# Attention of the first two batches ahead of the dense layer, and each decoded weight chunk used for both batches

## The chip, the cores and the metric

The kernel runs on one core of a Trainium2 chip. The metric is the device time of one execution in microseconds (us). The engines are TensorE (PE in the rows; PEld is its weight load), ScalarE (ACT), VectorE (DVE), GpSimd (POOL) and SyncE (SP); SPq, ACTq and POOLq are their instruction queues where they issue DMAs.

## The reference

Four batches of 448 tokens pass through attention with a sigmoid, a dense layer with a leaky rectifier, and a layer of eight experts, one for each token.

```python
def _attn_ref(q, k, v):                     # (4, 12, 448, 64) each
    scores = scale * np.matmul(q, k.transpose(0, 1, 3, 2)) - np.log(S)
    return np.matmul(1.0 / (1.0 + np.exp(-scores)), v)

def _moe_ref(x, w_in, w_out):               # 1792 x 768, 768 x 2048, 2048 x 768
    h = x @ w_in
    return np.maximum(0.01 * h, h) @ w_out

def _moe2_ref(x, w_gate, w_output_gate, w1, w2):   # 8 experts, 768 x 1024 x 768
    e_idx = np.argmax(x @ w_gate, axis=1)          # one expert for each token
    out[mask] = gate_w * eom * (np.maximum(x[mask] @ w1[e], 0.0) @ w2[e])
```

w_in and w_out arrive as 64-bit floats. All other inputs are 32-bit.

## The kernel before, in words

*Products.* Each product of float32 values is three fast matmuls: `mm3` multiplies the high part of the weights (`whi`) with the high and the low part of the activations, and the low part (`wlo`) with the high part. A weight chunk is up to six blocks of 128x128. ScalarE casts it to `whi`, VectorE subtracts to get `wlo`; five raw chunks, three high and three low ones fit.

*Decoding.* A chunk of w_in or w_out is read as pairs of 32-bit words into one of five places (`r64x`, `r64big`), in two pieces of up to three blocks. ScalarE shifts the exponent (`dw`), VectorE puts the bits together in three operations (lines 1176, 1179, 1182), and the result goes into a raw tile and by a POOL DMA also into the scratch tensor `wscr`, from which later batches read it.

*Attention.* A batch has six pairs of heads. A pair has two halves, FRONT and BACK, of two score tiles each (`sc`). A half is one piece of PE work (`both`): the scores of this half, then the values (`pv`) of the half before. ScalarE makes the sigmoid (`at`) of a score tile, which frees it; two score tiles fit, and one tile of values. When a pair's values are complete, ScalarE casts them to the high part of x (`x0h`, `x1h`) and VectorE subtracts. Batch 0 loads k and q by rows and turns them on PE (`pst`); later batches load them in blocks of 32 columns, four DMAs for each of k and q, and turn them on VectorE (`kt`, `qt`). `TURNED` sets the first batch that does so.

*Stages.* `first_batches` lists the operations of attention 0, attention 1 and dense 0 (16 hidden tiles `f`, then 6 outer tiles `d`) with durations, due times and the tiles they use. `_Plan.order` plays them through with these durations: at each step the engine that is free first takes the ready operation with the earliest due time. Its order is the order in which the instructions are written, and each engine then works through its own in that order. Two banks (`ps_m`) hold dense sums. Behind it, `gen_M1` and `gen_M2` write the dense layer of batch 1, with the routing of batch 0 as a side job; then come the experts (`gen_M3`, `gen_M4`) beside attention 2, and the same for batches 2 and 3. At these, `ws.next` hands out the next chunk and loads four ahead.

Of the kernel before, what the change touches and what calls it, by code (L numbers as in the profile page):

```python
# [18 lines left out]
P = 128  # L19
# [15 lines left out]
class _Op:  # L35
    def __init__(self, eng, dur, fn, deps, new, due, lat):
        self.eng, self.dur, self.fn, self.deps, self.new, self.due, self.lat = eng, dur, fn, list(deps), new, due, lat
        self.start = self.end = None


class _Plan:
# [24 lines left out]
    def order(self):  # L66
# [29 lines left out]
        for op in self.ops:  # L96
            op.ready = 0.0
# [22 lines left out]
def kernel(  # L120
# [135 lines left out]
    IN_K, OUT_K = ksplit(KD), ksplit(KF)  # L256
    if wide:
# [5 lines left out]
        scr = dram.tile([KF * len(IN_K) + KD * len(OUT_K), P, KC * P], F32, name="wscr")  # L263
# [65 lines left out]
    def add_dense(first):  # L329
        slot = 0  # L330
        for src, src32, nout, ks in ((w_in, w_in32 if wide else None, KF, IN_K), (w_out, w_out32 if wide else None, KD, OUT_K)):
            for f in range(nout):
                for k0, k1 in ks:
                    kk = k1 - k0

                    def plain(src=src, k0=k0, k1=k1, f=f):
                        return src[k0 * P:k1 * P, f * P:(f + 1) * P].rearrange("(k p) n -> p k n", p=P)

                    def wide_src(src=src32, k0=k0, k1=k1, f=f):
                        return src[k0 * P:k1 * P, 2 * f * P:2 * (f + 1) * P].rearrange("(k p) n -> p k n", p=P)  # L340

                    def from_scr(slot=slot, kk=kk):
                        return scr[slot, :, :kk * P].rearrange("p (k n) -> p k n", k=kk)

                    if wide and first:
                        dec_src.append(wide_src)
                    ws.src.append((kk, P, from_scr if wide else plain))
                    slot += 1
# [21 lines left out]
    def after(n, f):  # L370
        later.append([n, f])
# [18 lines left out]
    TURNED = 1  # L390

    def load_nat(nm, b, p, by=(nc.sync, nc.sync)):
# [7 lines left out]
        elif b >= TURNED:  # L400

            a = nat_p.tile([P, S // SQ, SQ], F32, tag=nm, name=nm)
            for j in range(P // SQ):
                i, f = divmod(j * SQ, D)
                nc.sync.dma_start(a[j * SQ:(j + 1) * SQ], src[b, 2 * p + i, :, f:f + SQ].rearrange("(n t) d -> t n d", t=SQ))
# [161 lines left out]
    def gen_M2(b):  # L567
# [3 lines left out]
        for d in range(KD):  # L571
            ps = ps_m.tile([P, S], F32, tag="m", name="psm")
            for kk in range(KF):
                for k0, k1 in OUT_K:
                    if k0 == kk:
                        wh, wl = ws.next()
                        at = k0
                gh, gl = gs[kk]
                mm3(ps, wh[:, kk - at], wl[:, kk - at], gh, gl, kk == 0, kk == KF - 1)
# [3 lines left out]

    def rows_add(b, d):
        xh, xl = x2T[b]
        xf = at_p.tile([P, S], F32, tag="at", name="xf")
# [393 lines left out]
    def first_batches():  # L980
# [144 lines left out]
        x1 = attention_ops(1, D0, D_T * 0.93 / NP / NCH)  # L1125
# [10 lines left out]
        nj = KF * len(IN_K) + KD * len(OUT_K)  # L1136
        raws, stores, his, los = {}, {}, {}, {}

        def fresh(j):
# [7 lines left out]
            if j < nj and wide:  # L1147
                dws = pl.slot("dw", 1)
                lows, prev = [], []
                for h in range(2):  # L1150
# [33 lines left out]
                    o = pl.add(DMA, L_W64 * m / HC, get, new=(hs,), lat=LD_LAT)  # L1184
                    o = pl.add(ACT, 0.41, square, deps=(o, *prev[:1]), uses=(hs, *((dws,) if h else ())), new=() if h else (dws,))
# [3 lines left out]
                    lows.append(pl.add(DVE, 0.47, tail_bits, deps=(o,), uses=(hs, rs), due=DEC[0] + j * DEC[1]))  # L1189
# [11 lines left out]
            return [pl.add(DMA, L_W, get, deps=(stores[j - nj],) if wide else (), new=(rs,), lat=LD_LAT)]  # L1201
# [20 lines left out]
        R = D_T / (2 * KF * KD * T_M)  # L1222

        def product(j, k, ps, first, final, xs, xget, deps, prev):
# [3 lines left out]
            def mm():  # L1228
                if first:
# [5 lines left out]
                       new=(ps,) if first else (), due=D0 + nm * T_M * R)  # L1235
# [3 lines left out]
        gs, glo = [], []  # L1239
        j = 0  # L1240
        for f in range(KF):
            lo_op = chunk(j)
# [186 lines left out]
```

## Time and profile before

| | us |
|---|---|
| Time, median of 3 runs (lowest to highest) | 910.77 (908.49 to 912.19) |
| Profiled execution, own time | 910.09 |
| Its span in the trace | 908.5 |
| PE busy | 883.8 (97%) |
| DVE busy | 512.0 (56%) |
| ACT busy | 421.9 (46%) |
| PE's share of the chain that ended last | 80% |

The share of the span in which PE is busy is an average over stages, and matmuls are pipelined, so that a busy PE may still be slower than it could be; its matmuls are best counted by the distance between their starts. The granted clock (PEclk) is 1.00 at 2.4 GHz and 0.50 at 1.2 GHz.

### The profile page before, as it was taken

The page shows a single profiled execution, that of the slowest core. Times are in us where ns is not written, and L with a number is a line of the kernel's source. Part 1 is how long each engine was busy: PE and PEld are TensorE (multiplying, and loading weights), DVE is VectorE, ACT ScalarE, POOL GpSimd, SP SyncE. Part 2 cuts the span into 40 slices and gives each one's busy share as a digit, 9 for nine tenths or more (in the row PEclk, how much of TensorE's full clock was granted, in tenths as well). Part 3 has the DMA queues.
Part 4 walks back from the last instruction along what each step waited for, and adds up shares of the span by engine and source line. Part 5 has one row for each costly group of instructions (what it writes and reads, how often), then busy time and mean ns, then how long its engine had stood idle before and what let it go on. Part 6 is the DMA issues. An engine that isn't in the chain of part 4 may idle for free.

```text
span 908.5 us, 13034 instructions
## 1 busy us (share of the span) xinstructions
PE 883.8 (97%) x4592; PEld 738.1 (81%) x4592; DVE 512.0 (56%) x1006; ACT 421.9 (46%) x681; POOL 58.1 (6%) x94
## 2 busy tenths in 40 slices
PE   8789999999999999999999999999999999999996
PEld 6347778887999998978778888778999999899885
DVE  3857999962864336745434655433386432765433
ACT  5657677653454322355553656453244422233331
POOL 2100101100021000210000000000002100121000
PEclk9999999999999999999999999999999999999999
DMA  8987789782564343598546825242257434358433
GB/s 181 301 250 145 233 258 268 254 239 76 115 144 132 99 129 68 130 134 174 98 101 150 205 82 118 60 118 82 88 121 138 130 108 122 68 116 181 122 90 69
DMA packets 279940, 129.40 MB, mean 142 GB/s; under 512 B 189496, under 2 KB 264600, under 8 KB 279872
## 3 DMA queue, kind: packets, MB, share of 16 engines
q1 hardware_dynamic: 273824, 115.30, 52.9%
q0 software_dynamic: 4192, 12.89, 4.0%
q8 instruction: 37, 0.61, 0.3%
q10 hardware_dynamic: 1856, 0.34, 0.2%
q14 instruction: 31, 0.25, 0.1%
HBM read 104.77 MB, written 23.77 MB: 141 GB/s over the span
## 4 chain that ended last, share of the span: by engine, by line
PE 80%; issue 7%; DVE 6%; DMA 3%; ACT 1%; SPq 1%; POOL 0%; POOLq 0%; DVEq 0%; ACTq 0%
PE psm L362 22%; PE psm L363 21%; PE psm L364 21%; PE pv L454 7%; PE sc L441 7%; DMA r64big<-in_moe_w_in_dram 2%; DVE wlo L298 1%; DVE x2t L594 1%; DVE xf L587 1%; DVE gl L545 1%; SPq L411 1%; DVE g L542 1%; DMA kn<-in_k_dram 1%; PE lgT L564 1%; PE lgT L565 1%
## 5 line engine op out<-in xcount | busy, mean ns | idle before, releaser
L298 DVE TENSOR_TENSOR wlo<-raw,whi 128x768 fp32r<-128x768 f32 (+2 forms) x180 | 153.4, 855 | 83.6 <-ACT whi L290 81.9
L362 PE MATMUL psm<-gh,whi 128*128 128x448 f32 x528 | 192.8, 365 | 0.0
L364 PE MATMUL psm<-gh,wlo 128*128 128x448 f32 x528 | 191.4, 362 | 0.1
L363 PE MATMUL psm<-gl,whi 128*128 128x448 f32 x528 | 191.0, 362 | 0.0
L290 ACT CAST whi<-raw 128x768 fp32r<-128x768 f32 (+2 forms) x180 | 135.6, 753 | 90.7 <-PE psm L363 69.1
L362 PE MATMUL psm<-x0h,whi 128*128 128x448 f32 x288 | 107.0, 371 | 3.2 <-ACT x0h L1034 3.2
L362 PEld LDWEIGHTS psm<-gh,whi 128*128 128x128 f32 x528 | 99.1, 188 | 13.5 <-issue 6.5
L362 PE MATMUL psm<-x1h,whi 128*128 128x448 f32 (+1 forms) x288 | 106.3, 369 | 0.6 <-DVE g L542 0.6
L364 PEld LDWEIGHTS psm<-gh,wlo 128*128 128x128 f32 x528 | 99.0, 187 | 8.5 <-DVE wlo L298 1.4
L363 PE MATMUL psm<-x0l,whi 128*128 128x448 f32 x288 | 105.1, 365 | 0.6 <-DVE x0l L1038 0.6
L363 PE MATMUL psm<-x1l,whi 128*128 128x448 f32 (+1 forms) x288 | 105.1, 365 | 0.0
L364 PE MATMUL psm<-x1h,wlo 128*128 128x448 f32 (+1 forms) x288 | 105.0, 365 | 0.0
L364 PE MATMUL psm<-x0h,wlo 128*128 128x448 f32 x288 | 104.6, 363 | 0.0
L363 PEld LDWEIGHTS psm<-gl,whi 128*128 128x128 f32 x528 | 99.0, 187 | 6.2
L448 ACT ACTIVATE at<-sc,nbias 112x896 f32<-112x896 f32 x84 | 80.1, 1007 | 16.1 <-PE sc L441 16.0
L454 PE MATMUL pv<-at,vn 112*64 112x448 f32 x336 | 71.1, 552 | 0.0
L362 PEld LDWEIGHTS psm<-x0h,whi 128*128 128x128 f32 x288 | 54.2, 188 | 15.1 <-ACT x0h L1034 4.7
L362 PEld LDWEIGHTS psm<-x1h,whi 128*128 128x128 f32 x288 | 54.1, 188 | 7.5 <-DVE g L542 1.7
L363 PEld LDWEIGHTS psm<-x0l,whi 128*128 128x128 f32 x288 | 54.3, 188 | 4.7 <-DVE x0l L1038 1.4
L364 PEld LDWEIGHTS psm<-x1h,wlo 128*128 128x128 f32 x288 | 54.0, 187 | 4.5
L364 PEld LDWEIGHTS psm<-x0h,wlo 128*128 128x128 f32 x288 | 54.3, 188 | 3.9
L363 PEld LDWEIGHTS psm<-x1l,whi 128*128 128x128 f32 x288 | 54.0, 188 | 4.1
(224 smaller groups left out, 1041.2 us busy)
## 6 DMA issues: line engine op xcount, KB each, us to landing
raw<-wscr SPq DMA_DIRECT2D x66, 384.0 KB
raw<-in_moe_w_dram SPq DMA_DIRECT2D x32, 384.0 KB
raw<-in_moe_w_dram SPq DMA_DIRECT2D x48, 256.0 KB
raw<-wscr SPq DMA_DIRECT2D x36, 320.0 KB
r64big<-in_moe_w_in_dram SPq DMA_DIRECT2D x25, 384.0 KB
wscr<-raw POOLq DMA_DIRECT2D x22, 384.0 KB, 5.0
r64big<-in_moe_w_out_dram SPq DMA_DIRECT2D x20, 384.0 KB
vn<-in_v_dram SPq DMA_DIRECT2D x24, 224.0 KB
```

The costliest lines, as they stand in the source:

```text
L290: nc.scalar.copy(hi, self.got[i])
L298: nc.vector.tensor_sub(lo, r, hi.bitcast(F32))
L362: nc.tensor.matmul(ps, wh, xh, start=first, stop=False)
L363: nc.tensor.matmul(ps, wh, xl, start=False, stop=False)
L364: nc.tensor.matmul(ps, wl, xh, start=False, stop=last)
L411: by[i].dma_start(a[:, :, i, :], src[b, 2 * p + i].rearrange(how, c=NCH))
L441: nc.tensor.matmul(t[:, i, :S], kk[own, ks], qq[own], start=(n == 0), stop=(n == 2))
L448: nc.scalar.activation(a, sc[:, :, :S], ACTF.Sigmoid, bias=nbias[:TP], scale=scale)
L454: nc.tensor.matmul(pv[own], vn[:, i, c * D:(c + 1) * D], at[c][:, i], start=(c == 0), stop=(c == NCH - 1))
L542: after(AFTER[3], lambda g=g, t=t, ps=ps: nc.vector.tensor_max(g, t, ps))
L545: after(AFTER[2], lambda g=g, gh=gh, gl=gl: nc.vector.tensor_sub(gl, g, gh.bitcast(F32)))
L564: nc.tensor.matmul(lgT[b], wg_c[:, d], xh[:, d, :S], start=(d == 0), stop=False)
```

## The change

Attention 0 and 1 are planned one behind the other, and the dense layer of both batches behind them. The dense layer is cut into two halves of the inner features (eight hidden tiles each). In each half a decoded chunk of w_in serves batch 0 and then batch 1. The outer chunks of the first half also serve both; the partial sums are kept in SBUF (`parts`), batch 0's in tiles of the attention's `kh`, `kl` and `qh`, batch 1's in tiles of `at`. The outer chunks of the second half serve batch 0 alone; batch 1 takes them again from scratch (`AGAIN`) in the new `gen_M2b`, with the routing of batch 0 beside it. An outer chunk now has four blocks in place of five or six, in later batches too. Loads of chunks to be decoded have an earliest time in the plan (`LEAD`, `EVERY`). Batch 0 loads k and q in blocks and turns them on VectorE.

```diff
+    KQ, HF = KF // 4, KF // 2
...
+    ORDER = []
+    for h in range(2):
+        ORDER += [("in", f, 0, KD) for f in range(h * HF, (h + 1) * HF)]
+        ORDER += [("out", d, k0, k0 + KQ) for d in range(KD) for k0 in range(h * HF, (h + 1) * HF, KQ)]
...
+    AGAIN = [key for key in ORDER if key[0] == "out" and key[2] >= HF]
+    PLAIN = [("in", f, 0, KD) for f in range(KF)] + [("out", d, k0, k0 + KQ) for d in range(KD) for k0 in range(0, KF, KQ)]
+    SLOT = {key: i for i, key in enumerate(ORDER)}
...
-    TURNED = 1
+    TURNED = 0
...
-                for k0, k1 in OUT_K:
-                    if k0 == kk:
-                        wh, wl = ws.next()
-                        at = k0
+                if kk % KQ == 0:
+                    wh, wl = ws.next()
...
+    parts = {}
+
+    def gen_M2b(b):
+
+        gs = gT.pop(b)
+        x2T[b] = x_tiles(b, True)
+        xh, xl = x2T[b]
+        for d in range(KD):
+            ps = ps_m.tile([P, S], F32, tag="m", name="psm")
+            for kk in range(HF):
+                if kk % KQ == 0:
+                    wh, wl = ws.next()
+                gh, gl = gs[kk]
+                mm3(ps, wh[:, kk % KQ], wl[:, kk % KQ], gh, gl, kk == 0, kk == HF - 1)
+                yield 0.57
+            t = parts.pop((b, d))
+            nc.vector.tensor_add(t, ps, t)
+            nc.scalar.copy(xh[:, d, :S], t)
+            after(AFTER[0], lambda d=d, t=t: nc.vector.tensor_sub(xl[:, d, :S], t, xh[:, d, :S].bitcast(F32)))
...
-        xf = at_p.tile([P, S], F32, tag="at", name="xf")
+        xf = turn_p.tile([P, S], F32, tag="kq"[d % 2], name="xf")
...
-        DEC = (40.0, 5.0)
-        A_T = NP * 2 * (T_A + T_S2 + T_V2)
-        D0 = A0 + A_T
-        D_T = 2 * KF * KD * T_M + A_T
+
+        LEAD, EVERY = 16.0, 5.0
+        A_T = NP * 2 * (T_S2 + T_V2)
+        D0 = A0 + 2 * A_T
+        D_T = (2 * KF + 3 * HF) * KD * T_M
...
-        x1 = attention_ops(1, D0, D_T * 0.93 / NP / NCH)
+        x1 = attention_ops(1, A0 + A_T, A_T / NP / NCH)
...
+                    o.ready = D0 - LEAD + min(j, 4) * EVERY
...
-            return [pl.add(DMA, L_W, get, deps=(stores[j - nj],) if wide else (), new=(rs,), lat=LD_LAT)]
+            return [pl.add(DMA, L_W, get, deps=(stores[SLOT[AGAIN[j - nj]]],) if wide else (), new=(rs,), lat=LD_LAT)]
...
-                       new=(ps,) if first else (), due=D0 + nm * T_M * R)
+                       new=(ps,) if first else (), due=D0 + nm * T_M)
...
-        for f in range(KF):
-            lo_op = chunk(j)
+
+        def hidden(b, f, lo_op):
             ps = pl.slot("ps_m", 2)
             o = None
             for kk in range(KD):
-                o = product(j, kk, ps, kk == 0, kk == KD - 1, (x0,), lambda kk=kk: (xT[0][0][:, kk], xT[0][1][:, kk]),
-                            (lo_op, low_of[0][kk]), o)
+                o = product(j, kk, ps, kk == 0, kk == KD - 1, (xs[b],), lambda kk=kk: (xT[b][0][:, kk], xT[b][1][:, kk]),
+                            (lo_op, low_of[b][kk]), o)
...
+        def summed(b, d, h, jj, lo_ops):
+
             ps = pl.slot("ps_m", 2)
             o = None
-            for kk in range(KF):
-                for k0, k1 in OUT_K:
-                    if k0 == kk:
-                        lo_op = chunk(j)
-                        at, jj = k0, j
-                        j += 1
-                o = product(jj, kk - at, ps, kk == 0, kk == KF - 1, (gs[kk],), lambda kk=kk: gs[kk].t, (lo_op, glo[kk]), o)
-
-            def xhi(d=d, ps=ps):
+            for kk in range(HF):
+                f = h * HF + kk
+                o = product(jj + kk // KQ, kk % KQ, ps, kk == 0, kk == HF - 1, (gs[b, f],), lambda f=f: gs[b, f].t,
+                            (lo_ops[kk // KQ], glo[b, f]), o)
+            return ps, o
...
+        def first_half(b, d, ps, o):
+
+            new = ()
+            if b == 0:
+                nm = ("kh", "kl", "qh")[d % 3]
+                slot = pl.slot(nm, 2)
+                new = (slot,)
+            elif d % 2 == 0:
+                slot = pl.slot("at", 4)
+                new = (slot,)
+            else:
+                slot = acc[b, d - 1][0]
...
+            def keep():
+                if b == 0:
+                    slot.t = parts[b, d] = stk_p.tile([P, S], F32, tag=nm, name="part")
+                else:
+                    if d % 2 == 0:
+                        slot.t = at_p.tile([P, 2, S], F32, tag="at", name="part")
+                    parts[b, d] = slot.t[:, d % 2]
+                nc.scalar.copy(parts[b, d], ps.t)
+
+            o = pl.add(ACT, 0.45, keep, deps=(o, *((acc[b, d - 1][1],) if b and d % 2 else ())),
+                       uses=(ps, *(() if new else (slot,))), new=new)
+            acc[b, d] = (slot, o)
...
+        for h in range(2):
+            for f in range(h * HF, (h + 1) * HF):
+                lo_op = chunk(j)
+                for b in range(2):
+                    hidden(b, f, lo_op)
+                j += 1
+            if h == 0:
+                for d in range(KD):
+                    lo_ops = [chunk(j + i) for i in range(HF // KQ)]
+                    for b in range(2):
+                        first_half(b, d, *summed(b, d, h, j, lo_ops))
+                    j += HF // KQ
+        x2 = pl.slot("x0", 1)
+        before = None
+        for d in range(KD):
+            lo_ops = [chunk(j + i) for i in range(HF // KQ)]
+            ps, o = summed(0, d, 1, j, lo_ops)
+            j += HF // KQ
+            slot, kept = acc[0, d]
+
+            def total(d=d, ps=ps):
+                t = parts[0, d]
+                V.tensor_add(t, ps.t, t)
+
+            def xhi(d=d):
                 if d == 0:
                     x2T[0] = x_tiles(0, True)
-                nc.scalar.copy(x2T[0][0][:, d, :S], ps.t)
-
-            def xlo(d=d, ps=ps):
+                nc.scalar.copy(x2T[0][0][:, d, :S], parts[0, d])
+
+            def xlo(d=d):
                 xh, xl = x2T[0]
-                V.tensor_sub(xl[:, d, :S], ps.t, xh[:, d, :S].bitcast(F32))
-
-            end = D0 + nm * T_M * R
-            o = pl.add(ACT, 0.42, xhi, deps=(o, *((xlo2,) if xlo2 else ())), uses=(ps, *((x2,) if d else ())), new=() if d else (x2,), due=end + 1.0)
-            xlo2 = pl.add(DVE, 0.54, xlo, deps=(o,), uses=(ps, x2), due=end + 1.5)
+                V.tensor_sub(xl[:, d, :S], parts[0, d], xh[:, d, :S].bitcast(F32))
+
+            end = D0 + nm * T_M
+            o = pl.add(DVE, 0.62, total, deps=(o, kept), uses=(ps, slot), due=end + 1.0)
+            o = pl.add(ACT, 0.42, xhi, deps=(o, *((before,) if before else ())), uses=(slot, *((x2,) if d else ())), new=() if d else (x2,), due=end + 1.5)
+            before = pl.add(DVE, 0.54, xlo, deps=(o,), uses=(slot, x2), due=end + 2.0)
...
+            if b == 0:
+                add_dense(ORDER, True)
+                add_dense(AGAIN)
+            else:
+                add_dense(PLAIN)
+                add_dense(PLAIN)
...
         for nm in ("kn", "qn"):
-            load_nat(nm, 0, 0, (nc.sync, nc.scalar))
+            load_nat(nm, 0, 0, (nc.sync, nc.sync) if nm == "kn" else (nc.scalar, nc.scalar))
...
-            run(gen_M1(b + 1))
-            run(gen_M2(b + 1))
+            if b:
+                run(gen_M1(b + 1))
+                run(gen_M2(b + 1))
+            else:
+                run(gen_M2b(b + 1))
```

In the order of ScalarE's instructions stands what a pair of heads waits for. Before, around one pair of batch 0 (`dw` and `whi` are decoding, `x0h` the cast of a pair's values, `at` sigmoids):

```order
L1068 CAST kh<-pst 128x448
L1068 CAST qh<-pst 128x448
L1171 ACTIVATE dw<-r64big 128x384 x2
L1171 ACTIVATE dw<-r64x 128x384
L1034 CAST x0h<-pv 128x448
L448 ACTIVATE at<-sc,nbias 112x896 x2
L1171 ACTIVATE dw<-r64big 128x384 x3
L448 ACTIVATE at<-sc,nbias 112x896 x2
```

Now, first a stretch of batch 0, then one of batch 1:

```order
L1094 CAST kh<-kt 128x448
L1094 CAST qh<-qt 128x448
L1060 CAST x0h<-pv 128x448
L455 ACTIVATE at<-sc,nbias 112x896 x4
L1094 CAST kh<-kt 128x448
L1094 CAST qh<-qt 128x448
```

```order
L1060 CAST x1h<-pv 128x448
L455 ACTIVATE at<-sc,nbias 112x896 x2
L1197 ACTIVATE dw<-r64big 128x384 x3
L1197 ACTIVATE dw<-r64x 128x384
L455 ACTIVATE at<-sc,nbias 112x896 x2
L1094 CAST kh<-kt 128x448
L1094 CAST qh<-qt 128x448
```

Decoding has moved out of batch 0's pairs into those of batch 1; the cast of the values still stands ahead of the sigmoids.

In SP's queue, before, the loads of decoding (line 1157) begin among the pairs of batch 0 (`kn`, `qn`, `vn` are loads of k, q and v):

```order
L411 DMA kn<-in_k_dram 112x4x64 x2
L1157 DMA r64x<-in_moe_w_in_dram 128x3x256
L411 DMA qn<-in_q_dram 112x4x64 x2
L1157 DMA r64big<-in_moe_w_in_dram 128x3x256
L411 DMA kn<-in_k_dram 112x4x64 x2
L1157 DMA r64big<-in_moe_w_in_dram 128x3x256
L399 DMA vn<-in_v_dram 112x2x256
```

Now the first of them (line 1183) stand behind the loads of batch 1's fourth pair:

```order
L412 DMA qn<-in_q_dram 32x14x32 x4
L1183 DMA r64x<-in_moe_w_in_dram 128x3x256
L1183 DMA r64big<-in_moe_w_in_dram 128x3x256 x2
L404 DMA vn<-in_v_dram 112x8x64
L412 DMA kn<-in_k_dram 32x14x32 x4
L412 DMA qn<-in_q_dram 32x14x32 x4
L1183 DMA r64big<-in_moe_w_in_dram 128x3x256 x2
L1183 DMA r64x<-in_moe_w_in_dram 128x3x256
L1183 DMA r64big<-in_moe_w_in_dram 128x3x256
L412 DMA kn<-in_k_dram 32x14x32 x4
```

Each load of k and q waits until VectorE has turned the pair two before it.

On PE, before, a new hidden tile takes a new chunk (numbers are those of the buffers):

```order
L362 MATMUL psm_923<-x0h_349,whi_506 128x448
L363 MATMUL psm_923<-x0l_350,whi_506 128x448
L364 MATMUL psm_923<-x0h_349,wlo_521 128x448
L362 MATMUL psm_963<-x0h_349,whi_903 128x448
L363 MATMUL psm_963<-x0l_350,whi_903 128x448
L364 MATMUL psm_963<-x0h_349,wlo_909 128x448
```

Now the same chunk is used for batch 0 and then for batch 1:

```order
L369 MATMUL psm_1293<-x0h_338,whi_923 128x448
L370 MATMUL psm_1293<-x0l_339,whi_923 128x448
L371 MATMUL psm_1293<-x0h_338,wlo_935 128x448
L369 MATMUL psm_1335<-x1h_814,whi_923 128x448
L370 MATMUL psm_1335<-x1l_815,whi_923 128x448
L371 MATMUL psm_1335<-x1h_814,wlo_935 128x448
```

## Rows read from the trace of the kernel before

**Rows 1.** Busy time by stage: stretch, length, engines, PEclk, DMA share, GB/s

```profile
0.00:75.50 75.50, 61.74 (x359) 35.52 (x359) 42.26 (x88) 45.55 (x70) 10.08 (x27) 0.95 0.92 233
75.50:222.60 147.10, 147.10 (x776) 117.99 (x775) 121.02 (x247) 93.34 (x158) 14.54 (x26) 1.00 0.76 221
222.60:342.50 119.90, 119.60 (x600) 110.26 (x599) 63.04 (x123) 45.76 (x75) 7.21 (x9) 1.00 0.47 117
```

**Rows 2.** PE in order of time: start, length, line, tiles, count [idle before]

```profile
15.51 0.60 PE L424 MATMUL pst<-ident,qn 112*128 112x112 f32 x4
...
62.20 1.72 PE L454 MATMUL pv<-at,vn 112*64 112x448 f32 x8
63.85 0.46 PE L441 MATMUL sc<-qh,kh 64*112 64x448 f32 x2
...
65.26 1.72 PE L454 MATMUL pv<-at,vn 112*64 112x448 f32 x8
...
216.64 0.36 PE L362 MATMUL psm<-gh,whi 128*128 128x448 f32 x1
...
222.44 0.36 PE L364 MATMUL psm<-gh,wlo 128*128 128x448 f32 x1
```

**Rows 3.** ACT in order of time, two places in the first batch

```profile
20.39 1.92 ACT L448 ACTIVATE at<-sc,nbias 112x896 f32<-112x896 f32 x2
...
67.03 0.53 ACT L1034 CAST x0h<-pv 128x448 fp32r<-128x448 f32 x1 [2.04 <-PE pv L454]
67.46 1.91 ACT L448 ACTIVATE at<-sc,nbias 112x896 f32<-112x896 f32 x2
```

**Rows 4.** PE in order of time, same two places

```profile
21.46 0.46 PE L441 MATMUL sc<-qh,kh 64*112 64x448 f32 x2 [0.99 <-ACT at L448]
...
22.36 0.46 PE L441 MATMUL sc<-qh,kh 64*112 64x448 f32 x2
...
23.15 1.72 PE L454 MATMUL pv<-at,vn 112*64 112x448 f32 x8
```

**Rows 5.** Groups by line, to 222.6 us: busy us, mean ns, idle before

```profile
L1179 DVE SCALAR_TENSOR_TENSOR raw<-dw,raw 128x384 uint32<-128x384 uint32 x56 | 30.4, 555 | 0.9
L1171 ACT ACTIVATE dw<-r64big 128x384 f32<-128x384 f32 x45 | 24.8, 560 | 23.8 <-DMA r64big<-in_moe_w_in_dram 9.1 <-DVE raw L1179 5.8 <-DMA r64big<-in_moe_w_out_dram 3.9
L1182 DVE SCALAR_TENSOR_TENSOR raw<-r64big,raw 128x384 uint32<-128x384 uint32 x45 | 23.9, 552 | 0.3
L1215 DVE TENSOR_TENSOR wlo<-raw,whi 128x768 fp32r<-128x768 f32 x24 | 22.9, 954 | 5.1 <-ACT whi L1211 4.4
...
L1176 DVE TENSOR_SCALAR raw<-dw 128x384 uint32<-128x384 uint32 x56 | 19.1, 353 | 7.5 <-ACT dw L1171 7.4
...
L1257 DVE TENSOR_TENSOR g<-t,psm 128x448 f32<-128x448 f32 x16 | 9.8, 611 | 2.0 <-ACT t L1253 2.0
```

**Rows 6.** Waits of ACT, to 222.6 us: total us, times, longest

```profile
ACT dw L1171 <- DVE raw L1179: 12.2, 7, 2.8
...
ACT dw L1171 <- DMA r64big<-in_moe_w_in_dram: 9.1, 5, 4.6
```

**Rows 7.** SP's DMA issues in order of time

```profile
0.92 0.74 SPq L411 DMA_DIRECT2D kn<-in_k_dram  x1
...
67.40 2.12 SPq L405 DMA_DIRECT2D kn<-in_k_dram  x4
```

**Rows 8.** PE in order of time, start of the program

```profile
4.69 0.95 PE L424 MATMUL pst<-ident,kn 112*128 112x112 f32 x4
...
7.92 0.46 PE L441 MATMUL sc<-qh,kh 64*112 64x448 f32 x2
```

**Rows 9.** PE in order of time, three waits in the first batch

```profile
27.05 0.58 PE L441 MATMUL sc<-qh,kh 64*112 64x448 f32 x2 [2.17 <-ACT at L448]
...
42.21 0.60 PE L424 MATMUL pst<-ident,qn 112*128 112x112 f32 x4 [1.57 <-DVE ql L1072]
...
57.52 0.47 PE L362 MATMUL psm<-x0h,whi 128*128 128x448 f32 x1 [1.89 <-ACT x0h L1034]
```

**Rows 10.** Busy time behind the first of these waits

```profile
28.00:30.00 2.00, 2.00 (x12) 1.08 (x10) 1.62 (x4) 1.21 (x3) 0.00 (x0) 0.50 1.10 393
```

More of the change, by code (lines that the diff above doesn't have):

```diff
@@ L38, in __init__ @@
         self.start = self.end = None
+        self.ready = 0.0
 class _Plan:
@@ L95, in order @@
         done = []
-        for op in self.ops:
-            op.ready = 0.0
         while len(done) < len(self.ops):
@@ L254, in ksplit @@
         return [(n * j // m, n * (j + 1) // m) for j in range(m)]
-    IN_K, OUT_K = ksplit(KD), ksplit(KF)
+    KQ, HF = KF // 4, KF // 2
+    assert KD <= KC and KQ <= KC
+    ORDER = []
[5 more added lines that the diff above has]
+    SLOT = {key: i for i, key in enumerate(ORDER)}
     if wide:
@@ L327, with add_dense, plain, wide_src @@
     ereg = {}
[L329 to L348, printed above, removed]
+    def add_dense(keys, first=False):
+        for key in keys:
+            nm, f, k0, k1 = key
+            src, src32 = (w_in, w_in32 if wide else None) if nm == "in" else (w_out, w_out32 if wide else None)
+            def plain(src=src, k0=k0, k1=k1, f=f):
+                return src[k0 * P:k1 * P, f * P:(f + 1) * P].rearrange("(k p) n -> p k n", p=P)
+            def wide_src(src=src32, k0=k0, k1=k1, f=f):
+                return src[k0 * P:k1 * P, 2 * f * P:2 * (f + 1) * P].rearrange("(k p) n -> p k n", p=P)
+            def from_scr(slot=SLOT[key], kk=k1 - k0):
+                return scr[slot, :, :kk * P].rearrange("p (k n) -> p k n", k=kk)
+            if wide and first:
+                dec_src.append(wide_src)
+            ws.src.append((k1 - k0, P, from_scr if wide else plain))
     def e_view(w, e, k0, k1, f):
@@ L1268, in first_batches @@
             o = pl.add(ACT, 0.47, ghi, deps=(o,), uses=(g_,), new=(gg,))
-            glo.append(pl.add(DVE, 0.54, glo_, deps=(o,), uses=(g_, gg)))
-            j += 1
-        x2 = pl.slot("x0", 1)
-        xlo2 = None
-        for d in range(KD):
+            glo[b, f] = pl.add(DVE, 0.54, glo_, deps=(o,), uses=(g_, gg))
+        def summed(b, d, h, jj, lo_ops):
             ps = pl.slot("ps_m", 2)
             o = None
-            for kk in range(KF):
-                for k0, k1 in OUT_K:
-                    if k0 == kk:
-                        lo_op = chunk(j)
-                        at, jj = k0, j
-                        j += 1
-                o = product(jj, kk - at, ps, kk == 0, kk == KF - 1, (gs[kk],), lambda kk=kk: gs[kk].t, (lo_op, glo[kk]), o)
-            def xhi(d=d, ps=ps):
+            for kk in range(HF):
[3 more added lines that the diff above has]
+            return ps, o
@@ L1312, in first_batches @@
             ws.got[jj] = (his[jj].t, los[jj].t) if jj < stage[1] else raws[jj].v
-        gT[0] = None
+        gT[1] = [gs[1, f].t for f in range(HF, KF)]
     A_PE = NP * 2 * C_E + 2 * C_V + 7.5
@@ L1360 @@
         for b in range(0, B, 2):
-            for i in range(2):
-                add_dense(b + i == 0)
+            if b == 0:
[4 more added lines that the diff above has]
+                add_dense(PLAIN)
             for i in range(2):
```

24 lines of the change are left out of this document (12 added, 12 removed).

## Prediction

> **What bounds the kernel now.** I read the table of stages first [rows 1]. TensorE is busy in every slice behind 75.5 us, and its clock is 1.00 there; VectorE, with 121.0 of 147.1 us, and ScalarE, with 93.3, both have room. Only the first stage is loose: 61.7 busy us of 75.5 at a mean clock of 0.95. So the time is TensorE's work plus what that engine loses at the start, and a change can gain only by cutting one of the two.
>
> The timeline of TensorE gives the price of the work. Twenty-nine steps lie between the two dense matmuls at 216.64 and 222.44, so one costs 0.200 us [rows 2]. A dense batch has 2·16·6·3 = 576 of them: 115.2 us. Half an attention pair is 1.41 us of scores and 1.65 us of values, 3.06 together [rows 2]; two batches have 24 halves: 73.4 us. Four transposes take 0.6 us [rows 2], so the twelve groups of batch 0 take at most 7.2 us. The first dense batch and both attentions therefore need 115.2 + 73.4 + 7.2 = 195.8 us, and they end at 222.6: 26.8 us are lost, nearly all before 75 us. The stage from 222.6 to 342.5, of 119.9 us, is the second dense batch (115.2) and the routing's matmuls (4.7) [rows 1].
>
> **What goes and what stays.** All 1152 dense matmuls of the two batches stay, and so do the 24 halves. The transposes on TensorE go (at most 7.2 us); VectorE turns that batch instead. Batch 1 takes the second half of the inner features last, and reads those outer chunks from the scratch tensor. Decoding, which is VectorE's load, is spread over twice the matmuls, but the trace shows no TensorE wait that this could cure: behind 75.5 us it has none [rows 1]. So the question is how much TensorE loses in twelve attention pairs run one after the other, against 26.8 + 7.2 = 34.0 us now.
>
> **A pair alone.** The order of ScalarE keeps the cast of the previous pair's values (x0h) ahead of the first sigmoids of the next pair. At the undisturbed place of the trace, scores start at 63.85, values behind them at 65.26, the cast follows at 67.03 and the sigmoids at 67.46: 3.61 us from scores to sigmoids [rows 2, 3]. A second pair of score tiles can't start before the sigmoid has emptied the first: at the other place the sigmoids start at 20.39, the scores at 21.46 and 22.36, the values at 23.15 [rows 3, 4]: 2.76 us on. With 1.65 us of values a pair takes 3.61 + 2.76 + 1.65 = 8.02 us, of which TensorE works 6.12. I take 8.0; with decoding between, as now, it is longer.
>
> **The sum of the new start.** (1) First scores: now at 7.92, 3.2 us behind the first transposes [rows 8]. The first load is now four issues of some 0.53 to 0.74 us [rows 7] in place of one, so about 8.5. ScalarE's first sigmoids stand behind the cast of pair 1's k, and the next ones behind that of its q. The loads are in SP's order: nine issues of 0.6 us from 0.92 on, and 3.0 us from the issue's end to use (0.92 + 0.74 to 4.69 [rows 7, 8]), then some 0.6 us to turn (an estimate from g, of the same size [rows 5]) and 0.5 to cast [rows 3]: 10.5. Two sigmoids take 1.9 us, q is there four issues later at 12.9, two more sigmoids, and pair 1's scores start near 15. (2) Pairs 1 to 4: 32.0, pair 5 with two groups of values behind it 8.0 + 1.65; one wait for the fourth pair's q, which VectorE turns before it frees the values' bank, about 1: 57.7. (3) Batch 1: six pairs of 8.0 are 48.0. Less 1.7, since no values stand behind its first scores; plus twice twelve dense matmuls ahead of scores, 4.8; plus 2.9 for the last pair's values and cast. Ahead of the second sigmoids ScalarE has three and four decode casts of 0.56 us [rows 5] in two pairs, and a mean wait of 12.2/7 = 1.7 us for VectorE in each [rows 6]; a pair hides about 1.1 us of this. That adds 1.7 + 1.7 − 1.1 = 2.3 and 2.2 + 1.7 − 1.1 = 2.8. Together 59.1, ending at 116.8. Here TensorE has done 51 of the dense matmuls: the rest of its first tiles waits for batch 1's last pair, and only two banks hold dense sums.
>
> (4) Dense: 1152 − 51 = 1101 at 0.200 are 220.2, and the routing 4.7: 341.7. (5) Waits for decode loads. They now stand in SP's queue behind k and q loads that wait for free buffers. Now ScalarE waits 9.1 us for w_in's [rows 6]. Between 0 (all hidden by the dense fill) and 9 I take 3: 344.7. The end of this part is 342.5 now, so +2.2 us; the profiled execution has 910.1 us, which becomes 912.3, and 913 with the 1 us below. The median of the runs shown, 910.8, lies 0.7 above that execution, inside the runs' own spread, so nothing is added for it.
>
> **What lies beside the dense part.** Two hidden tiles take TensorE 7.2 us. For them VectorE decodes a chunk of four blocks and subtracts one of six. A three-block piece costs 0.353 + 0.555 + 0.552 = 1.46, the subtraction 0.95, and four operations on hidden features like g 0.61 each [rows 5]. No row shows a one-block piece: it costs between a third of 1.46 (0.49) and all of it; I take 0.8, nearer to the third. The sum is 5.7 (5.3 to 6.3): hidden. An outer chunk is 4.8 us of TensorE against 1.46 + 0.8 + 0.7 = 3.0. In the last part of batch 0 each chunk serves only 2.4 us: 28.8 us in all. By the order five decodings are left (11.3), twelve subtractions (8.4), and six sums and six remainders of about 0.61 (7.3): 27. The new addition of two halves has no row: it lies between 0.35 (a smaller shift) and 0.95 (the larger subtraction), and I take g's 0.61, which reads a bank too. This part is level with TensorE, so a stall of 0 to 4 us may show there; I take 1. Without the lead of decoded chunks, all twelve decodings late, it would be 7·2.3 = 16 us.
>
> From 342.5 on nothing is added but smaller outer chunks (2.4 us instead of 3.0 to 3.6), whose loads keep four chunks of lead: 0 (−1 to +2).
>
> **The rivals.**
> *The attention runs tighter (faster).* If the dense fill hides the decode casts and all loads come in time, the terms 2.3, 2.8, 1 and 3 go: 344.7 turns into 335.6, 6.9 us ahead of now: 903. For it: the dense tiles stand just where ScalarE is late. Against it: ScalarE's order is fixed, and the 8.0 us chain holds without any decoding.
> *The clock falls in the gaps (slower).* In each pair TensorE stands still for some 1.5 us behind the values. The trace has waits of 2.17 and 1.89 us [rows 9] and behind the first the granted clock is 0.50, its lower level of 1.2 GHz [rows 10]; behind the wait of 1.57 us the four transposes take 0.60 us, as at 15.51 [rows 2, 9], so it stayed up. At half clock 1.41 us of scores take 2.8; of these 1.4 us some 1.2 show, as ScalarE is late anyway. In ten of the twelve pairs that is 12 us: 925. It decides from the point where most pairs lose the clock. The Trainium skill (TensorE: Matmul & The Clock Gate, "A second HAM failure mode: psum-queue depth-cycling") tells of a kernel that stands idle briefly between groups of matmuls while it cycles through PSUM banks, and loses throughput to falling and rising again. By that rule this rival is the result, some 925; by the row of 1.57 us it is not. No run here shows the repeated gap yet.
> *The decode loads are late (slower).* SP issues in order, and a k load that waits for its buffer holds the weights behind it. If ScalarE waits as long as now and the dense fill hides nothing, the 3 us above become 9.1: 919.
> *The change doesn't do what it says.* Chunks shared by both batches relieve VectorE, but in the part where a chunk serves one batch alone TensorE still waits for VectorE: 4 to 9 us more (of the 16 above), 917 to 922.
>
> **How the numbers follow.** The forecast, 907 to 918, has a chance of 0.50; the tighter attention 0.18; the clock 0.12; late loads 0.14; VectorE at the end 0.06. About 0.5% is what a measurement of this kernel can tell from no change: 906.2 to 915.3. All of the first rival but a tenth is faster, and a little of the forecast: 0.19. Of the forecast two thirds and some of the others' edges fall within: 0.42. The rest is slower, 0.39. The range, 903 to 924, leaves out half of the clock's case and the best of the first rival.
>
> **What would show it.** Right: pairs of 8 us in batch 0 with waits of TensorE for "at" of about 1.5 us; batch 1's attention over at 112 to 122 us; from there dense matmuls every 0.20 us without waits; the first expert matmul at 341 to 350 us. The clock's case shows 0.50 in most pairs; late loads show as ScalarE's "dw" waiting for DMA between 55 and 110 us; the last rival as TensorE waiting for "wlo" around 280 to 310 us. The forecast is wrong if pairs in batch 0 take under 7 or over 9.5 us, or if the dense stretch has waits over 5 us in total.

## The result and the profile after

The changed kernel takes 920.55 us (median of 4 runs, 918.58 to 921.66); the kernel before took 910.72 on the same chip (4 runs, 908.49 to 912.19). The ratio is 1.0108, 95% interval 1.0078 to 1.0137: slower by some 1%. The forecast was 913, with a range of 903 to 924. The profiled execution took 921.62 us, with a span of 919.9.

The table of stages of the kernel after, cut where the work changes: batch 0's attention, batch 1's, the dense part, all the rest. Columns as in [rows 1].

```profile
0.00:63.72 63.72, 50.93 (x270) 24.31 (x270) 23.70 (x47) 34.43 (x48) 5.64 (x19) 0.89 0.66 111
63.72:125.50 61.78, 53.88 (x295) 27.88 (x294) 37.31 (x76) 41.07 (x62) 4.40 (x8) 0.94 0.84 218
125.50:350.90 225.40, 224.11 (x1122) 208.52 (x1122) 160.68 (x378) 100.47 (x200) 18.30 (x33) 1.00 0.50 146
350.90:919.90 569.00, 556.19 (x2863) 474.32 (x2862) 288.59 (x562) 239.86 (x392) 32.67 (x40) 1.00 0.51 117
```

The reader sees that the dense part is full (224.1 busy of 225.4 us, clock 1.00), as its like was before [rows 1], and that the two attention stretches are not, with mean clocks of 0.89 and 0.94. The first expert matmul starts at 350.9 where it was at 342.5 [rows 1]: 8.4 us of the loss lie ahead of it, 3.0 behind (569.0 in place of 566.0).

TensorE in order of time, in batch 0 of the kernel after: scores of first and second halves, and the values behind second halves.

```profile
7.57 0.46 PE L448 MATMUL sc<-qh,kh 64*112 64x448 f32 x2 [0.30 <-ACT qh L1094]
...
12.32 0.46 PE L448 MATMUL sc<-qh,kh 64*112 64x448 f32 x2 [3.02 <-ACT at L455]
...
17.26 0.46 PE L448 MATMUL sc<-qh,kh 64*112 64x448 f32 x2
...
21.94 0.46 PE L448 MATMUL sc<-qh,kh 64*112 64x448 f32 x2 [1.54 <-ACT at L455]
...
23.66 3.25 PE L461 MATMUL pv<-at,vn 112*64 112x448 f32 x8
26.84 0.51 PE L448 MATMUL sc<-qh,kh 64*112 64x448 f32 x2
...
31.56 0.46 PE L448 MATMUL sc<-qh,kh 64*112 64x448 f32 x2 [1.54 <-ACT at L455]
...
33.27 1.72 PE L461 MATMUL pv<-at,vn 112*64 112x448 f32 x8
34.93 0.46 PE L448 MATMUL sc<-qh,kh 64*112 64x448 f32 x2
...
54.11 0.52 PE L448 MATMUL sc<-qh,kh 64*112 64x448 f32 x2
...
63.72 0.46 PE L448 MATMUL sc<-qh,kh 64*112 64x448 f32 x2
```

In each of the pairs 1 to 5 TensorE stands 1.54 us before the second scores, waiting for the first sigmoids. What follows is of two kinds. Behind 31.56 the eight values take 1.72 us, as in [rows 2], and the pair 8.09 us (26.84 to 34.93). Behind 21.94 they take 3.25, and the pair 9.58. The other pairs start at 34.93, 44.54 and 54.11: 9.61 and 9.57 behind falls at 40 and 50 us, and 9.61 for the last without a fall, as it carries a second group of values. Busy time of the engines in two stretches behind such waits shows why (PEclk is the sixth figure behind the comma, without the counts in brackets):

```profile
24.00:26.00 2.00, 2.00 (x8) 0.47 (x4) 0.68 (x2) 1.75 (x3) 0.00 (x0) 0.50 0.67 123
...
34.00:36.00 2.00, 2.00 (x16) 1.10 (x14) 1.06 (x2) 1.37 (x3) 0.00 (x0) 1.00 0.01 1
```

The granted clock is at its lower level (0.50, 1.2 GHz) in one and at the upper (2.4 GHz) in the other; only the first lost it. The mean clocks of the four executions lie between 0.985 and 0.988, so it fell in all of them. ScalarE has the order that the prediction spoke of [rows 3]:

```profile
20.44 0.53 ACT L1060 CAST x0h<-pv 128x448 fp32r<-128x448 f32 x1 [3.22 <-PE pv L461]
20.87 3.96 ACT L455 ACTIVATE at<-sc,nbias 112x896 f32<-112x896 f32 x4
```

It is idle for 3.22 us with scores ready since 18.7, since the cast of the previous pair's values stands first. Its waits for the decode loads of w_in add up to 4.6 us (52 to 130 us; total, times, longest), those of `r64big` to 3.3, against 9.1 in [rows 6]:

```profile
ACT dw L1197 <- DMA r64big<-in_moe_w_in_dram: 3.3, 3, 1.8
...
ACT dw L1197 <- DVE raw L1205: 1.5, 1, 1.5
...
ACT dw L1197 <- DMA r64x<-in_moe_w_in_dram: 1.3, 2, 1.0
```

Two of them stand ahead of the last cast of batch 0 and of the sigmoids behind it, for which TensorE waits in batch 1's first pair; the clock falls behind that wait as well (values of 2.68 us). ScalarE, then TensorE:

```profile
63.63 0.55 ACT L1197 ACTIVATE dw<-r64x 128x384 f32<-128x384 f32 x1 [0.97 <-DMA r64x<-in_moe_w_in_dram]
65.14 0.54 ACT L1197 ACTIVATE dw<-r64big 128x384 f32<-128x384 f32 x1 [0.96 <-DMA r64big<-in_moe_w_in_dram]
65.59 0.51 ACT L1060 CAST x0h<-pv 128x448 fp32r<-128x448 f32 x1
```

```profile
67.07 0.46 PE L448 MATMUL sc<-qh,kh 64*112 64x448 f32 x2 [1.87 <-ACT at L455]
...
69.36 2.68 PE L461 MATMUL pv<-at,vn 112*64 112x448 f32 x8
```

### The profile page after: what moved, and what is told of

It reads as the page before. It is cut to its first block, busy times and chain, and to the rows that moved or that the text cites. A ratio compares the mean times of both kernels' runs of the same rounds, so it can differ in the third digit from the quotient of the medians.

```text
span 919.9 us, 13152 instructions
## 1 busy us (share of the span) xinstructions
PE 885.1 (96%) x4544; PEld 735.0 (80%) x4544; DVE 510.3 (55%) x1062; ACT 415.8 (45%) x701; POOL 61.0 (7%) x100
## 4 chain that ended last, share of the span: by engine, by line
PE 74%; issue 7%; DVE 4%; DMA 2%; ACT 1%; SPq 1%; POOL 0%; POOLq 0%; DVEq 0%; ACTq 0%
PE psm L369 21%; PE psm L371 21%; PE psm L370 21%; PE pv L461 5%; PE sc L448 4%; DMA raw<-in_moe_w_dram 2%; DVE wlo L308 1%; DVE x2t L619 1%; SPq L562 1%; DVE xf L612 1%; PE lgT L571 1%; PE lgT L572 1%; DMA r64big<-in_moe_w_in_dram 1%; DVE gl L552 0%; DVE g L549 0%
## 5 line engine op out<-in xcount | busy, mean ns | idle before, releaser
L308 DVE TENSOR_TENSOR wlo<-raw,whi 128x512 fp32r<-128x512 f32 (+1 forms) x170 | 132.9, 785 | 77.2 <-ACT whi L300 76.9
L300 ACT CAST whi<-raw 128x512 fp32r<-128x512 f32 (+1 forms) x170 | 118.5, 699 | 94.8 <-PE psm L370 60.1
L461 PE MATMUL pv<-at,vn 112*64 112x448 f32 x336 | 77.3, 593 | 0.0
```

Source lines behind the costliest of these rows:

```text
L300: nc.scalar.copy(hi, self.got[i])
L308: nc.vector.tensor_sub(lo, r, hi.bitcast(F32))
L461: nc.tensor.matmul(pv[own], vn[:, i, c * D:(c + 1) * D], at[c][:, i], start=(c == 0), stop=(c == NCH - 1))
```

## Experiments

The theory: a pair's first sigmoids stand behind the cast of the previous values, this opens a hole of 1.54 us per pair, and some of the holes drop the granted clock, 1.5 us more each. The rivals: the loads (decode loads late, small k and q loads), VectorE, the order of decoding. Ratios are to the kernel before on the same chip, with 95% intervals; the experiments ran on several chips, so two kernels are compared by their ratios.

**1. The hole filled, in both batches.**

```
+        FILL = 6
...
+            for _ in range(FILL):
+                nc.tensor.matmul(more[0][:, :P], ident, ident, start=True, stop=True)
...
                             part(back)
+                            if cs == FRONT:
+                                fill()
```

> The changed kernel with six extra matmuls of the identity (128x128, into a PSUM bank that stands unused in this part) behind the values of every first half of a pair, where TensorE waits 1.54 us for the sigmoids. They compute nothing that is used. Clock theory: the wait alone makes a pair of 8.0 us, and the 9.6 us of five or six pairs come from the granted clock, which falls behind the wait. With the wait filled no pair shows 0.50, pairs of batch 0 take 8.0 to 8.1 throughout, and 5 to 6 falls of 1.5 us each go: 911 to 914 us. Rival (the 9.6 us pairs wait for loads, casts or their own chain, and the clock only follows): the pairs still alternate between 8.1 and 9.6, and the time stays at 919 to 922. Third: the extra matmuls run into the scores behind them: slower than 921.

Measured: 922.16 us, 1.0135 (1.0109 to 1.0162): no gain, a miss for the total; it lies at the edge of the rivals' cases. TensorE in order of time, and two stretches:

```profile
20.37 1.60 PE L1043 MATMUL fill<-ident 128*128 128x128 f32 x12
...
28.39 1.60 PE L1043 MATMUL fill<-ident 128*128 128x128 f32 x12
...
30.00 0.46 PE L448 MATMUL sc<-qh,kh 64*112 64x448 f32 x2
...
62.83 0.46 PE L448 MATMUL sc<-qh,kh 64*112 64x448 f32 x2 [2.46 <-ACT at L455]
...
73.45 1.60 PE L1043 MATMUL fill<-ident 128*128 128x128 f32 x12
74.81 0.45 PE L369 MATMUL psm<-x0h,whi 128*128 128x448 f32 x1
```

```profile
24.00:26.00 2.00, 2.00 (x14) 0.90 (x12) 0.66 (x2) 1.77 (x3) 0.00 (x0) 1.00 0.75 137
...
126.00:129.00 3.00, 3.00 (x10) 2.65 (x9) 3.00 (x9) 0.38 (x1) 0.00 (x0) 0.50 0.00 0
```

The mechanism is as expected: from pair 1 on the clock stays at 1.00 in batch 0, pairs follow each other by 8.02 us, and batch 1 starts at 58.9 and not at 63.7. These 4.8 us are three falls of some 1.5. They are given back further on, in three places. The first decode casts wait for their loads (1.93 and 0.59 us), and TensorE waits 2.46 us at 62.8 (1.87 in the changed kernel), where the clock falls in both. The extra matmuls also stand in batch 1, at five places from 73.45 to 114.96, where dense matmuls come next: those start 1.36 to 1.55 us later each, 7.0 us together, against waits of 2.4 us at the same places in the changed kernel and one fall there (at 101 us). And behind the wait for the last pair (1.29 us in both kernels) the clock falls at 126, where in the changed kernel it did not. So at batch 1's first routing matmul only 0.7 us are left (350.8 against 351.5), and the tail took 1 more. The run shows the price of the clock in batch 0, but not that of the hole, and its total says nothing of either.

**2. Scores and values planned apart.** The planner knew one step of scores with the values behind them, so for it the sigmoids and the cast came ready together.

```
-                    o = pl.add(PE, T_S2 + (T_V2 if back else 0.0), both, deps=deps, uses=uses, new=new, due=due(cs[1]))
+                    o = pl.add(PE, T_S2, first, deps=ready, uses=four, new=sc, due=due(cs[1]))
                     if back:
-                        last = o
+                        last = pl.add(PE, T_V2, lambda back=back: part(back),
+                                      deps=(o, back[2], *(back[6][c] for c in back[7])),
...
```

> The changed kernel with the planner's step of scores and values cut into two steps, so that it knows that scores are ready before the values behind them end; its price of a k or q load is 1.8 in place of 1.3, which keeps the start of ScalarE's order as it is. By this the first sigmoids of a pair stand ahead of the cast of the previous pair's values. Chain theory: the cast ahead of the sigmoids is what costs, a pair falls from 8.1 to 9.6 us to about 6.5 (1.41 scores, wait for the second score tile, cast and remainder before the values' bank is free), the 1.54 us wait goes and the clock stays at 1.00 from 25 us on; batch 1's attention ends at 100 to 106 us and not at 125.5: 895 to 903 us. Rival A (loads: SP issues eight loads of k and q of 0.5 us per pair, and the decode loads among them): pairs stay above 7.5 us, 910 to 920. Rival B (ScalarE's decode casts and the weights come late once the attention is shorter): batch 0 gains, but TensorE waits for dw, whi or wlo behind 90 us and half of it is lost: 905 to 912.

Measured: 893.7 us, 0.9827 (0.9811 to 0.9844): faster than both kernels, and 1 us below the range expected. ScalarE in order of time:

```profile
42.20 1.91 ACT L455 ACTIVATE at<-sc,nbias 112x896 f32<-112x896 f32 x2 [0.24 <-PE sc L448]
44.41 0.53 ACT L1060 CAST x0h<-pv 128x448 fp32r<-128x448 f32 x1 [0.31 <-PE pv L461]
45.26 1.91 ACT L455 ACTIVATE at<-sc,nbias 112x896 f32<-112x896 f32 x2 [0.32 <-PE sc L448]
```

TensorE's waits up to 130 us in the same run:

```profile
PE sc L448 <- ACT at L455: 2.7, 2, 1.6
PE hot L1034 <- POOL ident L203: 1.5, 1, 1.5
PE pv L461 <- DVE x0l L1064: 1.4, 1, 1.4
PE pv L461 <- DMA vn<-in_v_dram: 0.7, 1, 0.7
```

The sigmoids now stand ahead of the cast. Of the waits for "at" two are left up to 130 us, and second halves start at 38.16, 44.29 and 50.42: 6.13 us a pair, where its work is 6.12. Batch 1's first scores come at 47.4 (63.7 before the cut). Of these 16.4 us 2.8 lie ahead of pair 1, where the first loads come in another order too; 13.6 lie in the five pairs behind it, where ScalarE's order differs by the place of the cast alone. Batch 1's first routing matmul comes 26.5 us earlier (325.0 against 351.5). The other 10 us lie in batch 1, where the cut also moved the decode casts, from the first pair (63.6) to the fourth (68.4); what each of the two is worth there was not taken apart. Neither rival is seen in batch 0: the same k and q loads keep up with pairs of 6.13 us. In batch 1 one late load is left: ScalarE waits 1.94 us for it at 68.4, ahead of sigmoids, TensorE 1.04 us behind it, and the clock falls there.

**3. The control: the load price alone.** The cut also raised the planner's price of a load.

```
-L_QK, L_V, L_W64, L_W, LD_LAT = 1.3, 0.95, 1.55, 1.45, 2.0
+L_QK, L_V, L_W64, L_W, LD_LAT = 1.8, 0.95, 1.55, 1.45, 2.0
```

> The changed kernel with only the planner's price of a k or q load raised from 1.3 to 1.8, as in the run with scores and values planned apart, and nothing else: a control. ScalarE still has the cast of the previous values ahead of a pair's first sigmoids. Chain theory: pairs stay at 8.0 to 9.6 us and the time at 917 to 922. Rival (the price, by another order of the loads, made the 27 us gain): 893 to 905.

Measured: 925.87 us, 1.0164 (1.0146 to 1.0182). Some 4 us above what was expected, on the side away from a gain. The wait of 1.54 us is there in five pairs as before, this one with the clock lost behind it, so the price isn't what cured them:

```profile
30.94 0.46 PE L448 MATMUL sc<-qh,kh 64*112 64x448 f32 x2 [1.54 <-ACT at L455]
...
33.05 2.92 PE L461 MATMUL pv<-at,vn 112*64 112x448 f32 x8
```

**4. The same cut in the kernel before.**

> The kernel before the change with the same cut of the planner's step (nothing else). If the same chain on ScalarE costs there too, its first 75 us get shorter: of the 26.8 us that TensorE loses there, up to half, 897 to 905 us. If the transposes, the decode loads and the decode casts set the pace there, as ScalarE's waits for them say, it stays at 908 to 913. Together with the run of the changed kernel so cut it tells whether the change itself is worth something once the chain is out of the way: by the count of matmuls and transposes it saves at most 7 us of transposes, so 0 to 8 us between the two.

Measured: 900.43 us, 0.9906 (0.9890 to 0.9923). TensorE in the old first stage is busy for 71.91 us, against 61.74 in [rows 1]:

```profile
0.00:75.50 75.50, 71.91 (x437) 45.70 (x438) 52.69 (x109) 56.02 (x87) 10.75 (x28) 1.00 0.87 231
```

So the coarse step cost the kernel before some 9 us as well. That it cost less there because dense matmuls lay in part of the holes is likely, but not shown. With the step cut in both, the change is worth 0.8% (0.9827 against 0.9906; the load price was raised in the changed kernel alone, where it gained nothing by itself); uncut it costs 1.1%.

**5. One part undone: batch 0 turned on TensorE again.**

```
-TURNED = 0
+TURNED = 1
```

> The changed kernel with one part undone: k and q of batch 0 are transposed on TensorE again, from two issues of 256-byte pieces each, in place of four and a VectorE transpose. Clock theory: the transposes of a pair (two times 0.6 us) stand in the wait of 1.54 us, keep the clock up and cost next to nothing: pairs of batch 0 take 8.0 to 8.3, 1 to 2 us come from the faster start: 912 to 917. Rival (TensorE's work counts): twelve groups of 0.6 us are added: 925 to 928. Rival (the start's loads are what the change lost): first sigmoids of pair 0 go ahead, 2 us from the start alone, and the pairs stay at 8.1 and 9.6: 917 to 919.

Measured: 916.24 us, 1.0078 (1.0061 to 1.0095). TensorE in order of time:

```profile
28.34 0.60 PE L431 MATMUL pst<-ident,qn 112*128 112x112 f32 x4
28.78 0.55 PE L431 MATMUL pst<-ident,kn 112*128 112x112 f32 x4
...
29.95 0.46 PE L448 MATMUL sc<-qh,kh 64*112 64x448 f32 x2 [0.63 <-ACT at L455]
```

First scores of pairs 1 to 5 are 8.02 us apart (17.27, 25.29, 33.30, 41.32, 49.33), with eight more matmuls in the first two holes and four in the third: here the transposes cost nothing, and behind the waits of 0.62 to 1.01 us that they leave the clock stays up. The last two holes have none; the wait at 45.99 leaves the clock up, the one at 54.00 loses it. By the ratios the kernel is some 3 us faster than the changed one (1.0078 against 1.0108), but the intervals touch; in the profiles batch 1's first scores come 3.2 us earlier (60.47 against 63.72).

**6. The same with the cut.** As experiment 5, in the kernel of experiment 2.

> The changed kernel with scores and values planned apart, and with batch 0 transposed on TensorE again. In the run without the cut the same step made the kernel 5 us faster, since the transposes stood in waits of 1.54 us. Theory (transposes cost nothing only where TensorE waits anyway): the pairs of batch 0 are now full, 6.13 us each with 6.12 of work, so two groups of 0.45 to 0.6 us make them 7.0 to 7.3, 5 to 7 us over six pairs, less some 1 us of the start: 897 to 901. Rival (VectorE's turning or the four load issues per tensor hold the attention back): it gets faster here too, 889 to 893.

Measured: 895.7 us, 0.9834 (0.9815 to 0.9853), not told apart from experiment 2, and between the two ranges expected. First scores of pairs 1 to 3:

```profile
13.61 0.46 PE L448 MATMUL sc<-qh,kh 64*112 64x448 f32 x2
...
20.79 0.46 PE L448 MATMUL sc<-qh,kh 64*112 64x448 f32 x2
...
27.98 0.46 PE L448 MATMUL sc<-qh,kh 64*112 64x448 f32 x2
```

A pair with two groups of transposes takes 7.18 us and not 6.13, so in full pairs they do cost 1.05. But pair 1 starts 0.9 us earlier and two waits of experiment 2 (1.4 and 0.7 us) are gone, and batch 1's first scores come at 48.0 against 47.4. I had counted 1 us for what comes back, and it was nearly all.

**7. The other part undone: decoding not held back.**

```
-o.ready = D0 - LEAD + min(j, 4) * EVERY
```

> The changed kernel with the other part undone: the decode loads are not held back, so the planner puts the first of them behind the third pair's loads and the decode casts among batch 0's sigmoids. Chain theory (the order on ScalarE sets the pace of the pairs, and a decode cast in it makes a pair longer): batch 0's pairs get to 9 to 11 us, since two or three casts of 0.56 us and their waits for loads stand ahead of sigmoids; batch 1's pairs get free of them; sum over both about level to 5 us worse: 919 to 927. Rival (the late decode loads are what the change lost, as batch 1 shows 5 us of waits of dw for DMA): 912 to 916.

Measured: 932.4 us, 1.0218 (1.0196 to 1.0241), beyond what was expected. ScalarE in order of time:

```profile
25.84 0.54 ACT L1197 ACTIVATE dw<-r64x 128x384 f32<-128x384 f32 x1 [8.42 <-DMA r64x<-in_moe_w_in_dram]
26.29 0.52 ACT L1060 CAST x0h<-pv 128x448 fp32r<-128x448 f32 x1
26.70 1.91 ACT L455 ACTIVATE at<-sc,nbias 112x896 f32<-112x896 f32 x2
```

At one decode cast that stands too early ScalarE waits 8.42 us with the sigmoids behind it, and TensorE waits 7.4 us for them. Holding the decoding back is worth some 10 us here (1.0218 against 1.0108); the change does not lose by it.

**8. The tail: outer chunks of four blocks in the kernel before.**

```
-IN_K, OUT_K = ksplit(KD), ksplit(KF)
+IN_K, OUT_K = ksplit(KD), [(i, i + 4) for i in range(0, KF, 4)]
```

> The kernel before with outer chunks of four blocks everywhere (four per output tile, as in the changed kernel, in place of three of five and six). From the first routing matmul of batch 1 to the end of the span the kernel before takes 565.4 us and the changed one 568.4. Theory of the tail (smaller chunks give ScalarE and VectorE less lead in batches 2 and 3): this stretch takes 568 to 570 here too. Rival (the tail's 3 us come from other stored places or from the loads of batch 2): it stays at 565 to 566. The first 343 us are told apart by the trace; a fourth decode piece per tile may add 0 to 5 us there.

Measured: 911.7 us, 1.0009 (0.9993 to 1.0024): not told apart from the kernel before. From batch 1's first routing matmul (344.3) to the end of the span (911.1) it takes 566.8 us, 1.4 more than before and 1.6 less than after, between the two cases expected. TensorE's waits in this stretch of this run begin with a row that the kernel before does not have:

```profile
PE psm L364 <- DVE wlo L298: 1.1, 3, 0.4
```

**9. The cut, with three chunks in batches 2 and 3.** The outer weights go to a scratch tensor in one row per output tile, so that chunks of five and six can be read.

```
+    OUT_K = ksplit(KF)
...
-    PLAIN = ... [("out", d, k0, k0 + KQ) for d in range(KD) for k0 in range(0, KF, KQ)]
+    PLAIN = ... [("out", d, k0, k1) for d in range(KD) for k0, k1 in OUT_K]
```

> The changed kernel with scores and values planned apart (893.7 us, 0.983 of before) and, in addition, batches 2 and 3 read the outer weights in three chunks of five and six blocks again, from a scratch tensor that holds an output tile's row in one piece; the decoding stays as it is. Theory of the tail: the stretch from batch 1's first routing matmul to the end falls from 570.2 to 565 to 567 us, and the time to 888 to 891. Rival (chunk size is not the cause): 892 to 896.

Measured: 894.24 us, 0.9808 (0.9789 to 0.9826), where the rival put it. The tail of its profile is 568.4 us against 570.2 in experiment 2, and no wait for "wlo" is left, but the times aren't told apart. Nor are the tails: with chunks of four they lie between 568.2 and 572.2 us in the changed kernel and in experiments 1 to 3 and 5 to 7, so 568.4 is no sign. What small chunks cost of the tail's 3.0 us is not shown; 1.4 is the difference of two single executions in experiment 8.

**10. The three together.** Experiments 2, 6 and 9 in one kernel.

> The changed kernel with scores and values planned apart, the outer weights of batches 2 and 3 in three chunks, and batch 0 transposed on TensorE again: the best of the parts together. The spans of the runs so far put the first two parts at 891.7 and the first and third at 892.2, each about 3 below the cut alone (895.2); if their gains add (a tail of 567 in place of 570, and no fall of the clock at 72 us), 889 to 892 us. Rival (both are within what one execution differs from another): 893 to 896.

Measured: 895.12 us, 0.9821 (0.9805 to 0.9838). The rival is right. The tail is 570.0 us with three chunks, against 568.5 in experiment 6 with four, the other way round than in experiment 9. What is left between these four kernels (893.7 to 895.7) is not told apart, and the cut alone holds the gain.

## Why the prediction was right, and which terms were not

The time lay in the range and slower was among the cases, but the forecast of 913 missed by 7.6 us, on its slower side, and 920.55 lies beyond the forecast's own band of 907 to 918. That the range held is in part luck: it reached up to 924 to take in half of the clock's case, to which the prediction gave 0.12. By its own signs the forecast was wrong: it named pairs over 9.5 us, and pairs 1, 3 and 4 took 9.57 to 9.61; batch 1's attention was over at 125.5 us and not by 122, the first expert matmul came at 350.9 and not by 350. By its own steps:

1. *What bounds the kernel* (TensorE's work plus what it loses at the start): right. Experiment 2 got 26.5 us out of the changed kernel ahead of the routing.
2. *First scores near 8.5, pair 1's near 15*: 7.57 and 17.26, 2.3 us late. As foretold, the first sigmoids stood behind the cast of pair 1's k, to 11.26; but the wait of 3.02 us that came of it took the clock, which I had not priced.
3. *A pair of 8.0 us*: this is the term that failed. The chain was right to 0.1 us wherever the clock stayed (8.09 here, 8.02 in experiments 1 and 5). But three of batch 0's five waits of 1.54 us dropped the clock, 1.5 us each. I had taken from the single wait of 1.57 us [rows 9] that such a wait leaves the clock up. The kernel before showed it once; repeated in every pair it did so in two of five. So batch 1 began at 63.7: 57.7, plus 2.3, plus 4.65 for three falls, less the 1 us for pair 4's q, which did not come.
4. *Batch 1, 59.1 us*: 61.8 to the last pair's matmuls. The clock fell there twice, behind waits of 1.87 at 67.1 and of 1.17 and 1.22 close together at 99.4 and 101.1: some 3 us, the same term once more.
5. *Dense matmuls at 0.200, no wait for VectorE at the end*: right, 225.4 us with 224.1 busy, and no row of TensorE waiting for "wlo". The rival of a VectorE that is late fell, and the 1 us taken for it did not come.
6. *Late decode loads, 3 us*: ScalarE waited 4.6 us for w_in's. As a term of its own it is not seen, but it did reach TensorE: both waits behind which batch 1 lost the clock stand behind a cast or sigmoids that a late decode load held up (waits of 0.97 and 0.96 us ahead of 67.1, and of 1.81 us ahead of 99.4). How much of item 4 is its doing was not tried. As the case that decides the time it fell: experiment 2 ran with the same loads in shorter pairs.
7. *The tail, 0 (−1 to +2)*: 3.0, and its cause stays open. The routing's waits for VectorE are some 1 us longer after (1.6 and 1.0 us for two products, 0.7 and 0.8 before), and why they are was not tried. The smaller chunks may have a share (1.4 us in experiment 8), but experiments 9 and 10 do not show one.

The terms add up: 6.0 us more at the start, 2.7 in batch 1, 0.5 in the dense part, 3 less for the loads, and 3.0 in the tail less the 1 us for VectorE are 8.2; the profiled execution, at 921.6, lies 8.3 above the prediction's 913.3. One sum of the prediction is short: the tighter attention's 903 leaves out the 1 us for VectorE that the forecast has.

The rival of the clock, priced at 925 with a chance of 0.12 for ten of twelve pairs at 1.2 us, came true in about half of them (six), at some 1.5 us each. The Trainium skill (TensorE: Matmul & The Clock Gate, "A second HAM failure mode: psum-queue depth-cycling") describes this: a kernel that stands briefly between groups of matmuls falls and rises again. By that rule the trace agrees, with three falls behind five waits of 1.54 us; it deserved more than 0.12.

What I did not see is that the order itself could be had otherwise. "ScalarE's order is fixed" was said against the tighter attention, and it was true of both kernels; but it came from one coarse step in the planner, and a tighter attention than that rival's is what experiment 2 shows, at 894.

## What to carry to other kernels

Where a chain over two engines leaves the bounding engine a small hole in every round, ask first which instruction stands at the head of the other engine's queue: here a plan that moved one cast behind two sigmoids was worth some 26 us (13.6 of them in five pairs where nothing else moved on ScalarE), and of the other edits tried alone on the same stretch none gained more than 5. A planner can only put in order what it sees apart; a step that holds two products, of which the first is wanted earlier, hides just the order that matters. And work taken off the bounding engine gains only if it did not lie in such a hole: the same transposes cost nothing in an attention with holes (its kernel was 3 to 5 us faster with them) and 1.05 us a pair in a full one, where waits that went took most of it back.

## What the hardware showed unexpectedly

Waits of the same length (1.54 us), with the same matmuls ahead of them, lost the granted clock at 21.94, 39.60 and 49.21 and kept it at 31.56 and 58.85; in the run with the price alone three of five such waits lost it (30.94, 40.57 and 58.23), and 22.91 and 50.23 kept it. The wait of 1.29 us ahead of the dense part kept it in the changed kernel and lost it in the run with the holes filled. Which wait loses it can't be read from its length alone in these runs; that a stretch with such waits loses it about every other time can (six of ten in these two runs).
